# Four sublayers of attention on one core: the second layer's first values turned by DMA, some reciprocals through DRAM, x turned by TensorE

## The chip, the cores and the metric

The kernel runs on one core of a Trainium2 chip. A core has TensorE (PE, matrix products into the eight banks of PSUM), VectorE (DVE), ScalarE (ACT), GpSimd (POOL), SyncE (SP, here only a queue that issues DMAs), and sixteen DMA engines between DRAM and its memory, SBUF. The metric is the device time of one execution in microseconds, as a median of runs.

## The reference

x is 2048 tokens by 1024, in bf16. Four sublayers follow each other, A, B, A, B, and each is added to its input. The second pair uses the same weights as the first; a pair is called a layer below. Both have 32 heads of 32. A is linear attention with a learned feature map, B is softmax attention, both take a layer-normed input.

```
qkv = norm(x) @ wqkv                                # both
A:  phi(t) = [softmax(t @ w_phi), softmax(-t @ w_phi)]
    kv = phi(k)^T v ;  z = sum over tokens of phi(k)
    o  = (phi(q) kv) / (phi(q) z + 1e-6)
B:  o  = softmax(q k^T / sqrt(32)) v
x   = x + o @ wo                                    # both
```

## The kernel before

x is kept in SBUF, transposed: `xT` has the 1024 features as 8 groups of 128 partitions, and the tokens along the free dimension. Tokens are worked in 4 chunks c of 512; heads in 8 groups g of 4 heads, 128 columns. Most matmuls are made four abreast (`mm`): a 128 x 32 piece of the weights for each 32 columns of PE, four pieces beside each other, each with 512 moving columns.

Each engine's order is set when the kernel is built. Every step is an `op` of class `Sched`, with an engine, an estimated duration, the steps it depends on, its buffers and a priority; a list scheduler then runs a model of the engines and takes, for each engine, the most urgent step that is ready by its estimates. It also places all buffers in one SBUF arena and the eight PSUM banks. Where it has nothing for PE it inserts matmuls that compute nothing (`idle`, `idle_acc`), so as not to let PE stop. Tables of numbers (LATER, VQ, KP, OUT, QA, AK and others) hold the priorities. Each engine then executes its list in order, and waits at the front of it.

The stages are these. `load_x` brings x: chunk 0's features half by transposing DMAs straight into `xT`, half by plain loads that PE turns with `nc.tensor.transpose`; the other chunks come by transposing DMAs. `fold_phi` multiplies w_phi into the key weights, and later into the query weights. `layernorm` needs sums over features, that is over partitions: either 64 matmuls with a constant matrix `onesD` (every partition then holds the sums), or, for the chunks in the table FEW, 16 matmuls that leave partial sums, which two small matmuls with `selm` then add up and spread (`sums`).

Sublayer A: keys and values for each chunk give `kv` and `z`; then `a_queries`, for each chunk and half of the heads, exponentials of the two signs, their denominators and numerators, and `a_out` the out-projection. Here reciprocals occur twice: the weight between the two signs (multiplied in at line 979) and one over the denominator (line 1020). Each is one row per head, four rows in each 32 partitions, and must reach 32 partitions per head. For that the row is split in a bf16 high and low part (`split_hl`, a CAST and a SCALAR_TENSOR_TENSOR on DVE), and `spread` multiplies with `selb` or `selr`, constant matrices, into PSUM, where DVE reads it.

Sublayer B: `b_k` and `b_q` make keys and queries transposed, `b_v` makes values with tokens on the partitions (the normed x is the stationary operand, the weights move, 256 columns for the first groups of heads), and `attention` runs 32 turns, each one group of heads and one chunk of queries. Its scores go to PSUM (line 1257). A unit is one 128 keys x 512 queries tile of scores. ACT makes exponentials of three or two units at once (line 1273, 1536 or 1024 wide); for some pairs of units DVE makes them by integer and float16 arithmetic (`exp_dve`, lines 1184 to 1203). The table COUNT says how many pairs DVE takes in each of the turns. PE multiplies with the values (line 1305). The denominators go to DRAM and come back as one load that broadcasts four rows to 32 partitions each:

```
bk = dma(prio, lambda ...: nc.sync.dma_start(
    out=r_v(), in_=at_d.unsqueeze(1).to_broadcast([4, 32, C512])), [aw], [d_b], kb=600)
```

Keys of layer 1's sublayer A are made within layer 0's attention, since its turns leave the chunks of x done one after the other.

Of the kernel before, what the change touches and what calls it, by code (L numbers as in the profile page):

```python
# [23 lines left out]
DH = 32  # L24
# [45 lines left out]
class Sched:  # L70
# [99 lines left out]
    def run(self):  # L170
# [32 lines left out]
        while left:  # L203
# [108 lines left out]
SBUF_ARENA = 172 * 1024 - 256  # L312
# [3 lines left out]
LONG = {"kT", "v", "slab", "slabk", "xn", "xn1", "kvacc", "kvm", "zm", "wnat"}  # L316
MODEST = {"slabk", "xn1", "e1", "vp1", "pkf", "lnw1", "w2o"}
NUMS = 2
LATER = ((26.4, 16.7, 25.9, 7.3), (18.7, 27.9, 15.9, 13.5))
VQ = (((0, 7.1), (50.5, 3.1), (53.0, 8.9)), ((15.5, 8.4), (75.8, 14.1), (152.2, 9.9)))  # L320
FULL = 5
OUT = (35.9, 27.1)
EARLY = (2.0, 4.0)
DUE = 0.0
BOOST = 25.0
EVAC = 30.0
QA = (105.3, 4.5)
# [4 lines left out]
         "rs": 8, "pkf": 1, "cden": 2, "part": 8, "w2r": 1,  # L332
# [8 lines left out]
HOST = ((), (16,), (11, 17), (0, 11, 21), (4, 10, 17, 24))  # L341
SIDE = (2, 4)
FEW = (((0, 1, 3), (0, 1, 2)), ((0, 1, 3), (0, 1, 2)))
WHOLE = 2
WK = (0.0, 1.5)
SLABD = (1, 3)
TOK = (0.0, 0.6, 0.61, 0.62)
SLOW = 6.0
HALF = 4
KGAP = (6.2, 2.2)  # L350
LATE = 15.3
KP = (0, 39.1, 45.7, 92.0, 62.9, 125.6, 160.1, 205.2)
BO = 225
OP0 = (240.8, 265.9, 289.4)
OGAP = (2.0, 2.6, 1.9)
COUNT = ((0, 0, 1, 2, 4, 4, 4, 3, 4, 3, 3, 4, 4, 4, 4, 3, 4, 3, 3, 4, 3, 2, 1, 2, 0, 2, 4, 2, 1, 2, 3, 3),
    (2, 4, 5, 4, 4, 4, 3, 5, 4, 4, 4, 4, 4, 4, 5, 4, 3, 5, 4, 4, 4, 4, 4, 4, 4, 2, 5, 4, 3, 1, 4, 4))
PAIRS = ((), ((0, 2),), ((0, 2), (1, 2)), ((0, 1), (0, 5), (1, 3)), ((0, 1), (0, 5), (1, 1), (1, 5)),
    ((0, 1), (0, 3), (0, 6), (1, 1), (1, 5)), ((0, 1), (0, 3), (0, 6), (1, 1), (1, 3), (1, 6)))
AK = ((0, 201.9), (1, 231.9), (2, 260.5))  # L360
OUT1 = ((177.6, 3.1), (195.5, 1.0), (246.4, 1.0))


def act_us(n):
    return n / 1200 + 0.064
# [10 lines left out]
def kernel(  # L376
# [52 lines left out]
    phi_t = const.tile([P, G * P], BF16, tag="phi")  # L429
    nc.vector.memset(phi_t[:].bitcast(U32), 0)  # L430
# [45 lines left out]
    gone = []  # L476
    qd = dram_p.tile([P, 2 * G * C512], BF16, tag="qd")
# [78 lines left out]
    def load_x():  # L556
        nb, nv = sb("xnat", TB, C512)
        nat = [dma(-24.0, lambda h=h: nc.gpsimd.dma_start(
            out=nv()[:, 2 * h:2 * h + 2, :],
            in_=A_x[0, 2 * h * P:2 * h * P + 2 * P, C512:D].rearrange("(t p) f -> p t f", p=P)),  # L560
            (), [nb], q="GQ", kb=256, issue=0.75) for h in range(2)]
        for lo, hi, prio, us, kb in ((0, 1, -24.0, 1.3, 128), (1, 2, -9.0, 1.3, 400), (2, NC, -8.0, 2.0, 800)):
            last = []
            for po in range(PO if lo else PO // 2):
# [4 lines left out]
                if not lo:  # L569
                    last[-1].slack = 0.5  # L570
# [153 lines left out]
    def phi():  # L724
        return phi_t[:].rearrange("p (g n) -> p g n", g=G)
# [867 lines left out]
```

## Time and profile before

| | |
|---|---|
| median of 3 runs | 2245.05 us (2242.07 to 2246.89) |
| the profiled execution | 2247.36 us, its span 2245.1 us |
| mean granted PE clock | 0.998 |
| ACT busy | 1985.7 us, 88% of the span |
| DVE busy | 1855.9 us, 83% |
| POOL busy | 197.0 us, 9% |
| DMA | 119.67 MB, mean 53 GB/s |

In the profile PE is TensorE's matmul, PEld its weight load, which lies beside the matmuls. A row names line, engine, operation, the result and operands with their tiles, partitions x elements and type, and then, after xcount, busy us and mean ns of one; after the second bar stands the engine's idle time just before such an instruction and what ended it. SPq, ACTq and POOLq are the queues in which an engine issues DMAs. A window is a stretch of the span; its row gives its length, each engine's busy time with its count, the granted PE clock, the DMA engines' busy share and GB/s. Matmuls are pipelined: the mean duration of one is not what it adds to the time, which is read from the starts of the following rows.

### The profile page before, as it was taken

Reading aid. Unit: us, or ns where it says so; the run is one execution under the profiler, and the core shown is the slowest. Engines: PE = TensorE matmul, PEld = TensorE weight load, DVE = VectorE, ACT = ScalarE, POOL = GpSimd, SP = SyncE. Lnnn points to the kernel's source line nnn. Section 1 sums busy time; section 2 is a strip of 40 time slices with the busy share of each in tenths; the row PEclk is TensorE's granted clock in tenths of the full one; section 3 lists DMA queues with packets and bytes.
Section 4 is the critical chain, followed back from the end, with each engine's and each line's share of the span. In section 5 each row is a group of like instructions: output and inputs, shape, how many; then the busy total and the mean of one; then the engine's idle time right before and its main releaser. Section 6 shows DMA issues by size and latency. Waiting matters only on the chain.

```text
span 2245.1 us, 82636 instructions
## 1 busy us (share of the span) xinstructions
PE 2176.1 (97%) x36788; PEld 872.2 (39%) x36788; DVE 1855.9 (83%) x2761; ACT 1985.7 (88%) x1939; POOL 197.0 (9%) x299
## 2 busy tenths in 40 slices
PE   7999999999999999999999999999999999999999
PEld 4554454444333333333333444433333333333333
DVE  7986873698899889677887788799999999988968
ACT  4436669999999999999998555999999999999998
POOL 1110000000001010121124200000000000100000
PEclk9999999999999999999999999999999999999999
DMA  9220101111122221222235100111111100211111
GB/s 207 49 81 3 33 24 42 41 34 34 51 57 88 74 73 54 64 96 73 78 110 152 59 5 10 36 37 38 36 29 29 35 24 19 73 31 35 47 36 38
DMA packets 121789, 119.67 MB, mean 53 GB/s; under 512 B 57752, under 2 KB 99800, under 8 KB 121432
## 3 DMA queue, kind: packets, MB, share of 16 engines
q1 hardware_dynamic: 102392, 56.64, 10.0%
q0 software_dynamic: 17424, 56.18, 8.7%
q8 instruction: 287, 4.70, 0.9%
q10 hardware_dynamic: 1616, 1.57, 0.2%
q14 instruction: 70, 0.57, 0.1%
HBM read 79.23 MB, written 14.14 MB: 42 GB/s over the span
## 4 chain that ended last, share of the span: by engine, by line
PE 28%; ACT 23%; DVE 9%; issue 5%; DMA 1%; SPq 0%; ACTq 0%; DVEq 0%
ACT arena L1273 22%; PE psum L530 14%; PE psum L1305 6%; PE psum L1257 6%; DVE arena L1203 2%; DVE arena L1184 1%; DVE arena L1196 1%; DVE arena L1201 1%; DVE arena L1193 1%; ACT arena L823 1%; DMA arena<-arena 1%; DVE arena L1370 1%; DVE arena L1198 1%; DVE arena L1057 1%; PE psum L994 0%
## 5 line engine op out<-in xcount | busy, mean ns | idle before, releaser
L1273 ACT ACTIVATE arena<-psum 128x1536 bf16<-128x1536 f32 (+1 forms) x1366 | 1668.5, 1446 | 12.0 <-PE psum L1257 7.1
L530 PE MATMUL psum<-arena 128*32 128x512 bf16 (+1 forms) x18432 | 1058.3, 358 | 12.5 <-DVE arena L836 2.7
L530 PEld LDWEIGHTS <-arena 128*32 128x32 bf16 x18944 | 459.8, 96 | 447.2 <-issue 175.7
L1305 PE MATMUL psum<-arena 128*32 128x512 bf16 x4096 | 628.1, 383 | 4.0 <-issue 2.0
L1305 PE MATMUL psum<-arena,ones_bf 128*32 128x512 bf16 x4096 | 628.1, 383 | 0.0
L1257 PE MATMUL psum<-arena 32*128 32x512 bf16 x4096 | 536.2, 383 | 27.2 <-ACT arena L1273 22.4
L1257 PEld LDWEIGHTS <-arena 32*128 32x128 bf16 x4096 | 158.4, 91 | 555.8 <-issue 549.0
L1184 DVE TENSOR_SCALAR arena<-psum 128x512 int32<-128x512 f32 x418 | 284.5, 686 | 101.7 <-PE psum L1257 90.3
L1203 DVE SCALAR_TENSOR_TENSOR arena<-arena 128x1024 int16<-128x1024 int32 x209 | 254.7, 1218 | 5.7 <-DVE arena L1201 0.4
L1305 PEld LDWEIGHTS <-arena 128*32 128x32 bf16 x4096 | 163.2, 95 | 227.8 <-issue 177.0
L1305 PEld LDWEIGHTS <-ones_bf 128*32 128x32 bf16 x4096 | 161.3, 95 | 22.3 <-issue 7.9
L705 POOL DMA_DIRECT2D arena<-in_B_wqkv_dram x46 | 42.2, 919 | 1248.6 <-PE psum L530 302.5
L1193 DVE TENSOR_SCALAR arena<-arena 128x1024 f16<-128x1024 int16 x209 | 143.8, 690 | 4.4 <-DMA arena<-arena 0.3
L1196 DVE TENSOR_TENSOR arena<-arena 128x1024 f16<-128x1024 f16 x209 | 142.6, 684 | 4.6
L1201 DVE TENSOR_TENSOR arena<-arena 128x1024 f16<-128x1024 f16 x209 | 142.6, 684 | 3.1
L1057 DVE CAST arena<-psum 128x512 bf16<-128x512 f32 x128 | 87.7, 685 | 57.6 <-PE psum L530 57.3
L823 ACT ACTIVATE arena<-psum 128x512 bf16<-128x512 f32 x80 | 43.0, 596 | 82.6 <-PE psum L530 66.7
L827 DVE TENSOR_REDUCE arena<-arena 128x32 f32<-128x1024 bf16 x64 | 77.0, 1214 | 33.3 <-ACT arena L823 33.2
L530 PE MATMUL psum<-xT,onesD 128*32 128x512 bf16 x1144 | 103.1, 381 | 1.3 <-DVE arena L836 0.7
L1321 DVE COPY arena<-psum 128x512 f32<-128x512 f32 x126 | 86.3, 685 | 15.4 <-PE psum L1305 15.0
L1198 DVE TENSOR_SCALAR arena<-arena 128x1024 f16<-128x1024 f16 x209 | 87.9, 422 | 1.7
L836 DVE TENSOR_TENSOR arena<-psum,arena 128x1024 bf16<-128x1024 f32 x64 | 77.4, 1219 | 13.3 <-PE psum L530 9.7
(124 smaller groups left out, 1383.6 us busy)
## 6 DMA issues: line engine op xcount, KB each, us to landing
arena<-rd SPq DMA_DIRECT2D x62, 256.0 KB
arena<-in_B_wqkv_dram POOLq DMA_DIRECT2D x58, 256.0 KB, 4.1
arena<-in_B_wo_dram POOLq DMA_DIRECT2D x40, 256.0 KB, 4.4
arena<-arena SPq DMA_DIRECT2D x256, 32.0 KB
arena<-wd_k POOLq DMA_DIRECT2D x32, 256.0 KB, 5.0
arena<-in_A_wqkv_dram POOLq DMA_DIRECT2D x32, 256.0 KB, 4.6
arena<-arena SPq DMA_DIRECT2D x96, 64.0 KB
arena<-arena SPq DMA_DIRECT2D x248, 2.0 KB
```

The source lines that it names most:

```text
L530: nc.tensor.matmul(out_[ks, :], lhsT=lhsT[:, ks], rhs=rhs, start=start, stop=stop, tile_position=(0, 32 * k), skip_group_check=True)
L1057: return op("DVE", dve_us(512), lambda: nc.vector.tensor_copy(out=dst(), in_=src()), [dep], bufs, prio)
L1184: o = op("DVE", dve_us(512), lambda: nc.vector.tensor_scalar(out=x_v()[:, k, :].bitcast(I32), in0=s_v()[:, x * C512:(x + 1) * C512], scala ...
L1193: last = op("DVE", 1024 / 1920 + 0.15, lambda: nc.vector.tensor_scalar(out=z(), in0=x_v().bitcast(I16).rearrange("p a (n two) -> p a n two ...
L1196: last = op("DVE", 1024 / 1920 + 0.15, lambda: nc.vector.tensor_tensor(out=u(), in0=z(), in1=z(), op=ALU.mult), [last], [z_b, u_b], prio + ...
L1198: last = op("DVE", 1024 / 3840 + 0.15, lambda: nc.vector.tensor_scalar(out=u(), in0=u(), scalar1=POW2_C[0], scalar2=POW2_C[1], op0=ALU.mul ...
L1201: last = op("DVE", 1024 / 1920 + 0.15, lambda: nc.vector.tensor_tensor(out=u(), in0=z(), in1=u(), op=ALU.mult), [last], [z_b, u_b], prio + ...
L1203: return op("DVE", dve_us(1024), lambda: nc.vector.scalar_tensor_tensor(out=y_v().bitcast(I16), in0=x_v().bitcast(I32), scalar=128.0 / BIT ...
L1257: nc.tensor.matmul(out=s_v()[:, x * C512:(x + 1) * C512], lhsT=kT[g][1]()[r, pp, d * P:(d + 1) * P], rhs=q_of[(qc, g)][1]()[r, (pp + j // ...
L1273: ex = op("ACT", act_us(w * C512), lambda s_v=s_v, e_v=e_v, w=w: nc.scalar.activation(out=e_v(), in_=s_v()[:, 0:w * C512], func=ACT.Exp, s ...
L1305: nc.tensor.matmul(out=a_v()[col:col + 32, :], lhsT=v_v()[:, kc % 4, o:o + DH] if what == 0 else ones_bf[:], rhs=ev()[:, x * C512:(x + 1) ...
L1321: cp = op("DVE", dve_us(512), lambda t_v=t_v, a_v=a_v: nc.vector.tensor_copy(out=t_v(), in_=a_v()), [last], [a_b, t_b], prio - 4)
```

## The change

1. **x turned by TensorE.** Chunk 0 comes by four plain loads on SP (two before on POOL's queue, for half the features), and 32 transposes on PE turn it, before 16 and four transposing DMAs; DVE and ACT move the result to `xT`. The first half of the key weights comes as four loads on SP, before as one on ACT's queue. The tile for w_phi now lies in the arena, and its loads wait for its memset there.
2. **Two head groups' V transposed.** In layer 1 (TURN) the values of groups 0 and 1 are made by the new `b_vt`: weights stationary, x moving, 512 columns, as keys are. The result goes to DRAM and back by a transposing DMA, so that tokens come on the partitions. `b_v` keeps the other groups. Group 0's is evacuated by ACT, group 1's by DVE.
3. **Reciprocals of two chunks through DRAM.** For chunks 1 and 2 of both layers (WIRE) the reciprocal of the denominator goes through the new `carry` in place of `split_hl` and `spread`: four stores of four rows, then seven loads which broadcast rows to 32 partitions (a load of four rows, and 3 + 1, 2 + 2, 1 + 3, since each quarter needs the heads in a rotated order). DVE's multiply reads them from SBUF. (Set in the table's first places, the weight between the signs could go that way too; those places are empty.)
4. **`exp_dve`** uses one buffer in place of two.
5. **Norms.** FEW changes: chunk 3 of layer 0's first norm and chunk 1 of layer 1's second norm are made with the 64 matmuls.
6. **Tables.** The priorities are other numbers; COUNT sums to 88 pairs in layer 0 (before 86) and 126 in layer 1 (before 123). In layer 1 seven turns have five pairs (before five) and one has six. The arena is 1 KB larger.

```diff
-LATER = ((26.4, 16.7, 25.9, 7.3), (18.7, 27.9, 15.9, 13.5))
+LATER = ((19.6, 38.4, 22.2, 22.6), (36.6, 33.2, 21.4, 16.4))
...
-FEW = (((0, 1, 3), (0, 1, 2)), ((0, 1, 3), (0, 1, 2)))
+FEW = (((0, 1), (0, 1, 2)), ((0, 1, 2, 3), (0, 2)))
+TURN = (1,)
+WIRE = (((), (1, 2)), ((), (1, 2)))
...
-COUNT = (...
-    (2, 4, 5, 4, 4, 4, 3, 5, 4, 4, 4, 4, 4, 4, 5, 4, 3, 5, 4, 4, 4, 4, 4, 4, 4, 2, 5, 4, 3, 1, 4, 4))
+COUNT = (...
+    (2, 4, 4, 4, 5, 4, 4, 4, 4, 4, 3, 4, 3, 5, 4, 4, 5, 4, 3, 5, 4, 4, 6, 4, 4, 3, 5, 4, 5, 2, 5, 1))
...
-    phi_t = const.tile([P, G * P], BF16, tag="phi")
-    nc.vector.memset(phi_t[:].bitcast(U32), 0)
...
     def load_x():
-        nb, nv = sb("xnat", TB, C512)
-        nat = [dma(-24.0, lambda h=h: nc.gpsimd.dma_start(
-            out=nv()[:, 2 * h:2 * h + 2, :],
-            in_=A_x[0, 2 * h * P:2 * h * P + 2 * P, C512:D].rearrange("(t p) f -> p t f", p=P)),
-            (), [nb], q="GQ", kb=256, issue=0.75) for h in range(2)]
+        nb, nv = sb("xnat", TB, D)
+        nat = [dma(-24.0, lambda t=t: nc.sync.dma_start(out=nv()[:, t, :], in_=A_x[0, t * P:t * P + P, :]),
+                   (), [nb], kb=256) for t in range(TB)]
...
-            ld.append([dma(-24.0, lambda: nc.scalar.dma_start(out=nv()[:, :, 0:C512], in_=A_w[:, :, col:col + C512]),
-                           (), [nb], q="AQ", kb=1024, issue=0.7)])
...
+    def carry(r_b, r_v, dep, prio, turn):
+        at_d = wd_v[len(sent)]
+        sent.append(prio)
+        st = [dma(prio, lambda a=a: nc.sync.dma_start(out=at_d[a], in_=r_v()[32 * a:32 * a + 4, :]),
+                  [dep], [r_b], kb=8) for a in range(4)]
+        got = []
+        for a in range(4):
+            b, v = sb("wb", C512, dt=F32)
+            got.append((b, v, [st[a], b, v]))
+        r = []
+        for a, (b, v, _) in enumerate(got):
+            n = turn * a % 4
+            for lo, hi, to in ((0, 4 - n, n), (4 - n, 4, 0)):
+                if hi > lo:
+                    o = dma(prio, lambda a=a, v=v, lo=lo, hi=hi, to=to: nc.sync.dma_start(
+                        out=v()[32 * to:32 * (to + hi - lo), :],
+                        in_=at_d[a, lo:hi].unsqueeze(1).to_broadcast([hi - lo, 32, C512])), [st[a]], [b], kb=260 * (hi - lo))
...
-        k_b, k_v, k = split_hl(r_b, r_v, l4, prio)
-        for a, (b_, v_, bm) in enumerate(spread(k_b, k_v, k, prio, selr)):
+        if c in WIRE[layer][1]:
+            wide_ = carry(r_b, r_v, l4, prio, 1)
+        else:
+            k_b, k_v, k = split_hl(r_b, r_v, l4, prio)
+            wide_ = spread(k_b, k_v, k, prio, selr)
+        for a, (b_, v_, bm) in enumerate(wide_):
             o_done[4 * hf + a] = op("DVE", ...
-                out=o_v()[:, 4 * hf + a, :], in0=nums[a][1](), in1=v_(), op=ALU.mult),
-                [bm, nums[a][2]], [b_, nums[a][0], o_b], prio)
...
+    def b_vt(g, c, prio, w, vT, banks, eng):
...
+        m = mmg2(pb, pv, lambda po: ww()[:, po, h * P:h * P + P], lambda po: xv()[:, po, :], fin, wd, [xb, wb], prio)
+        a_b, a_v = sb("kt", C512)
+        cp = evac(eng, a_v, pv, m, [pb, a_b], prio)
...
+        st = dma(prio, lambda: nc.sync.dma_start(
+            out=at_v.rearrange("(t p) n -> p t n", p=P), in_=a_v().rearrange("p (t n) -> p t n", t=TB)), [cp], [a_b], kb=256)
+        ld = dma(prio, lambda: nc.sync.dma_start_transpose(out=v_v(), in_=at_v), [st], [v_b],
+                 kb=256, issue=1.3)
...
+    phi_b, phi = sb("phi", G, P)
+    phi_0 = op("DVE", 0.5, lambda: nc.vector.memset(arena[:, phi_b.at // 2:phi_b.at // 2 + G * P].bitcast(U32), 0),
+               (), [phi_b], -30.0)
```

169 lines of the change are left out of this document (106 added, 63 removed), and 1 row of the table QUOTA.

## The prediction

> **What bounds the kernel now.** I read the page's busy line first, then a table of windows cut at the stages, then the groups by shape.
>
> The busy line gives each engine's busy time, its share of the span and its instructions:
>
> ```profile
> PE 2176.1 (97%) x36788; PEld 872.2 (39%) x36788; DVE 1855.9 (83%) x2761; ACT 1985.7 (88%) x1939; POOL 197.0 (9%) x299
> ```
>
> PE at 97% looks like the bound, but PE also runs matmuls that compute nothing, where the planner had no others. The windows decide it by stage: loading and first fold; layer 0's linear attention; its softmax attention; out-projection, norm and layer 1's linear attention (here the transition); layer 1's softmax attention.
>
> ```profile
> core 0: us, PE busy (x) PEld busy (x) DVE busy (x) ACT busy (x) POOL busy (x), PEclk, DMA share, GB/s
> 0.00:31.00 31.00, 16.29 (x370) 11.23 (x374) 21.21 (x49) 14.44 (x22) 4.57 (x12) 1.00 0.92 218
> 31.00:327.00 296.00, 290.26 (x6477) 152.22 (x6469) 242.06 (x319) 157.56 (x270) 26.78 (x54) 1.00 0.23 51
> 327.00:1213.00 886.00, 863.71 (x13701) 317.68 (x13694) 695.02 (x1025) 877.28 (x746) 123.08 (x172) 1.00 0.24 68
> 1213.00:1412.00 199.00, 196.38 (x3888) 95.80 (x3880) 155.92 (x220) 116.37 (x205) 18.87 (x35) 0.99 0.12 36
> 1412.00:2235.00 823.00, 803.40 (x12249) 292.19 (x12241) 737.28 (x1142) 817.69 (x692) 23.71 (x28) 1.00 0.13 35
> ```
>
> In the two linear stages PE is busy 98 to 99% and ACT under 60%: PE's sum of matmuls is the time. In the two softmax stages ACT is busy 99% (877 of 886, 818 of 823 us) and PE 98%, part of it filler. The loading stage is neither: PE 16 of 31 us, DMA share 0.92.
>
> ```profile
> L1273 ACT ACTIVATE arena<-psum 128x1536 bf16<-128x1536 f32 x946 | 1317.1, 1573 | 9.5 <-PE psum L1257 6.4 <-PE psum L1305 1.6 <-DVE arena L1203 0.5
> L1273 ACT ACTIVATE arena<-psum 128x1024 bf16<-128x1024 f32 x420 | 433.2, 1158 | 2.6 <-PE psum L1305 0.8 <-PE psum L1257 0.7 <-issue 0.5
> L1557 PE MATMUL psum<-xT,zero 128*32 128x512 bf16 x504 | 46.5, 379 | 0.0
> ```
>
> The exponentials take 1750 us of ACT and wait 12 us in all. The zero matmuls (x504) are one of the two kinds of filler. So the prices are ACT time in softmax stages, PE time in linear ones.
>
> **The change part by part.** The sum is made against the profiled execution's 2247.4 us (span 2245.1), which is 2.3 above the median of the runs, 2245.05.
>
> *Loading.* Before, chunk 0 of x came half by four transposing DMAs and half by plain loads turned on PE; now all of it comes plain. SP's first rows, before:
>
> ```order
> L566 DMA_TRANSPOSE xT<-in_A_x_dram 128x512 x4
> L735 DMA arena<-in_A_wqkv_dram 128x2x512 x4
> L566 DMA_TRANSPOSE xT<-in_A_x_dram 128x512 x7
> L709 DMA arena<-in_A_wqkv_dram 128x2x512 x8
> L788 DMA wd_k<-arena 128x8x512
> ```
>
> and after:
>
> ```order
> L567 DMA arena<-in_A_x_dram 128x1024 x4
> L740 DMA arena<-in_A_wqkv_dram 128x2x512 x8
> L594 DMA_TRANSPOSE xT<-in_A_x_dram 128x512 x6
> L719 DMA arena<-in_A_wqkv_dram 128x2x512 x8
> L594 DMA_TRANSPOSE xT<-in_A_x_dram 128x512
> ```
>
> Four transposes left the head of the queue, and the k weights' first half, which ACT's queue carried, joined SP behind x. The timeline and the DMA list (KB each, us from issue to landing):
>
> ```profile
> 0.75 5.34 SPq L566 DMA_TRANSPOSE xT<-in_A_x_dram  x4
> 3.03 2.33 POOL L1380 DMA_DIRECT2D phi_t<-in_A_w_phi_dram  x4
> 5.45 0.15 DVE L463 TENSOR_SCALAR hl<-hl 128x1 f32<-128x1 f32 x1
> 12.04 0.69 DVE L635 TENSOR_TENSOR arena<-xT 128x1024 bf16<-128x1024 bf16 x1 [6.44 <-DMA xT<-in_A_x_dram]
> 13.67 1.03 PE L748 MATMUL psum<-ident,arena 128*128 128x128 bf16 x8
> 15.00 1.28 DVE L635 TENSOR_TENSOR arena<-xT 128x1024 bf16<-128x1024 bf16 x2
> 18.99 0.74 PE L530 MATMUL psum<-phi_t,arena 128*32 128x128 bf16 x32
> 20.98 4.58 SPq L709 DMA_DIRECT2D arena<-in_A_wqkv_dram  x8
> ```
>
> ```profile
> arena<-in_A_x_dram POOLq DMA_DIRECT2D x2, 256.0 KB, 8.1
> phi_t<-in_A_w_phi_dram POOLq DMA_DIRECT2D x4, 16.0 KB, 8.8
> ```
>
> Four issues at 0.57 us (4.58 / 8) end at 3.0, and with 8.1 us to landing x is in at 11.1 at the latest, against a last square of x that starts at 15.0. Behind it, x and the first k half are 2 MB: 9.6 us at 218 GB/s, 11.6 us with 2 us of start, against 13.67 for the first turn of k. So the front could move by 2.1 to 3.9 us. What may hold it is phi: its loads now wait for a memset that stands behind DVE's constants (5.45). With 2.33 us of issues they are out by about 8.2, and 8.8 us later, at 17.0, they are there: before the fold at 18.99, 2 us of slack. I take **−2.5**, between −4.8 (the 8.1 us were two loads among many, the wait alone was 6.44) and +1 (phi late by the gain and more).
>
> *First linear stage.* One norm is made with the full sums (64 matmuls more, 16 sum matmuls and 2 spreads fewer), and 16 spreads of reciprocals go. Rows of the timeline for the prices:
>
> ```profile
> 1274.35 4.07 PE L530 MATMUL psum<-arena 128*32 128x512 bf16 x72
> 1278.35 0.40 PE L931 MATMUL psum<-arena,selb 32*128 32x512 bf16 x4
> 1412.47 1.93 PE L530 MATMUL psum<-arena 128*32 128x256 bf16 x64
> ```
>
> 72 matmuls of 512 columns in 4.00 us are 0.0556 each, a spread is 0.10, and 64 of 256 columns in 1.87 us (to the next row's 1414.34) are 0.029 each. Norm: 64 x 0.0556 − 16 x 0.0556 − 2 x 0.2 = +2.3; spreads 16 x 0.10 = −1.6. Together **+0.7**.
>
> *Layer 0's softmax stage.* By the order ACT has four fewer 1536-wide exponentials and four more 1024-wide ones (DVE takes 88 pairs, before 86): 4 x (1.573 − 1.158) = **−1.7**.
>
> *Transition.* 288 V matmuls of 256 columns go, 96 of 512 come: −8.4 + 5.3. Its own full norm +2.3 and 16 spreads −1.6. Sum **−2.4**. The 288 moved partly into the next stage, where 512-wide matmuls rise by 160 and 256-wide ones fall by 224: +8.9 − 6.5 on PE, which the fillers cover (264 zero and 748 norm-like matmuls in that stage are 56 us).
>
> *Layer 1's softmax stage.* Six exponentials narrow (123 to 126 pairs): 6 x 0.415 = −2.5. ACT's V casts:
>
> ```profile
> L1056 ACT CAST arena<-psum 128x256 bf16<-128x256 f32 x32 | 11.9, 384 | 7.9 <-PE psum L530 7.8
> L1056 ACT CAST arena<-psum 128x512 bf16<-128x512 f32 x10 | 5.9, 598 | 17.7 <-PE psum L530 17.6
> ```
>
> Seven casts of 0.37 fewer in this stage, one of 0.60 more: −2.0, of which I count half, since they stand where ACT still waits for PE. Sum **−3.5**.
>
> *V through DRAM.* SP's row in layer 1, before:
>
> ```order
> L1070 DMA arena<-arena 64x512
> L1071 DMA arena<-arena 64x512
> L1049 DMA arena<-arena 64x256 x16
> L1070 DMA arena<-arena 64x512
> L1071 DMA arena<-arena 64x512
> ```
>
> and after, from the fourth chunk's keys on:
>
> ```order
> L1083 DMA arena<-arena 64x256 x4
> L1165 DMA vd<-arena 128x4x128 x2
> L1167 DMA_TRANSPOSE arena<-vd 128x512
> L1165 DMA vd<-arena 128x4x128
> L1167 DMA_TRANSPOSE arena<-vd 128x512
> L1104 DMA arena<-arena 64x512
> L1105 DMA arena<-arena 64x512
> L1167 DMA_TRANSPOSE arena<-vd 128x512
> ```
>
> A store and a transposing load of V (L1165, L1167) now stand between the moves of keys (L1083) and of queries (L1104, L1105), so these wait in line behind V.
>
> ```profile
> 1495.38 2.42 SPq L1049 DMA_DIRECT2D arena<-arena  x4
> 1497.21 3.08 DMA arena<-arena
> ```
>
> The trip of V is a cast 0.6, the four key moves ahead 2.4, a store's issue 0.33 and landing 3.1, a transpose's issue 1.34 (5.34 / 4) and landing 3.1: 10.9 us. Between V's evacuation and its first use the order leaves PE work of 9.5 us (chunk 2) and 11.0 us (chunk 3). I count 0, at most +5: it happens at the ramp alone.
>
> *Reciprocals through DRAM.* In chunks 1 and 2 of both layers, each half's reciprocals are stored as four rows and loaded back broadcast to 32 partitions, seven loads of 256 KB by fours, 1 MB in all. DVE's row there in layer 0, before:
>
> ```order
> L1020 TENSOR_TENSOR arena<-arena,psum 128x512 x4
> L915 CAST arena<-arena 128x512
> L1033 TENSOR_TENSOR xT<-xT,psum 128x512
> L916 SCALAR_TENSOR_TENSOR arena<-arena,hl 128x512
> L1033 TENSOR_TENSOR xT<-xT,psum 128x512 x2
> L979 TENSOR_TENSOR arena<-arena,psum 128x512 x4
> ```
>
> and after (L1054 was L1020):
>
> ```order
> L1054 TENSOR_TENSOR arena<-arena 128x512 x2
> L622 SCALAR_TENSOR_TENSOR arena<-arena,hl,psum 128x512
> L1054 TENSOR_TENSOR arena<-arena 128x512
> L679 TENSOR_TENSOR arena<-psum,arena 128x512
> L1054 TENSOR_TENSOR arena<-arena 128x512
> L701 TENSOR_TENSOR arena<-xT,arena 128x1024 x2
> ```
>
> The multiplies moved back, one by one between the next norm's steps. Each waits for a DMA, and on DVE the norm stands behind it; on PE the out-projection waits for them. The kernel has one DMA of this kind, the softmax denominators' broadcast, also four rows to 128 partitions (issues: lowest, median, highest ns). While it alone runs the windows show:
>
> ```profile
> L1364 SPq DMA_DIRECT2D arena<-rd x62: 577/582/667, 369.6 to 2223.0; - x62
> 895.47:898.21 2.74, 2.74 (x42) 0.94 (x38) 1.57 (x2) 2.74 (x4) 0.00 (x0) 1.00 0.25 96
> 507.57:510.73 3.16, 3.16 (x53) 1.19 (x56) 3.09 (x5) 3.16 (x4) 0.00 (x0) 1.00 0.23 82
> 1506.42 0.47 SPq L1362 DMA_DIRECT2D rd<-arena  x1
> 1510.38 0.59 SPq L1364 DMA_DIRECT2D arena<-rd  x1
> ```
>
> The DMA share is 0.25, four of sixteen engines, and 256 KB take 2.74 to 3.16 us. A carry's 1 MB is thus 11.0 us if the split loads keep four engines busy, and 14.0 to 16.2 if loads of three and two rows use only three and two (one engine then carries 164 packets of 2 KB where a whole load gives it 32: 5.1 x). Two carries in a row are 22 to 32 us; ahead lie 0.6 of Exp, 4.0 from the store's issue to the load's (1506.42 to 1510.38), three more stores 1.0 and a load's issue 0.6, so 28 to 38.6. The order leaves 595 matmuls of 512 columns between the first half's Exp and the first use of the last product: 33.1 us. Late per chunk −5 to +5.5, middle about +0.4, times four chunks: **+2**, bounds 0 and +22.
>
> The Trainium skill ("DMA: Bandwidth & Descriptors", section "Why a DMA increments its semaphore by 16 and not by 1") says that a hardware-queued DMA is spread over the largest number of engines up to 16 that divides the outermost sizes of both sides, the lowest-numbered ones. The share of 0.25 agrees for four rows; for three and two no run here shows it. By it the carry is the longer one, and the sum would be that of the first rival.
>
> Sum: −2.5 + 0.7 − 1.7 − 2.4 − 3.5 + 2 = −7.4, so 2240.0 in the profiled execution and **2237.5** beside the median.
>
> **The rivals.** A: *carries late* (slower). Loads of three and two rows keep few engines, both halves share the same ones, every chunk is late by 5.5 us: +22 in place of +2, so −9.4 + 22 = +12.6, 2260 profiled, **2257.5**. It loses the gain from 2.4 us a chunk on and is slower than before by over 0.2% from 3.5 us ((9.4 + 4.5) / 4). For it: DVE and PE run in order, and the last product has 2 to 6 us of matmuls ahead of its reader. Against: other matmuls (next norm, keys) can stand ahead of the waiting one, and the 33.1 us are counted without any wait in between.
>
> B: *DVE becomes the bound* (slower). One pair on DVE:
>
> ```profile
> L1184 DVE TENSOR_SCALAR arena<-psum 128x512 int32<-128x512 f32 x418 | 284.5, 686 | 101.7 <-PE psum L1257 90.3 <-ACT arena L1273 4.9 <-ACT arena L1056 2.6
> L1193 DVE TENSOR_SCALAR arena<-arena 128x1024 f16<-128x1024 int16 x209 | 143.8, 690 | 4.4 <-DMA arena<-arena 0.3
> L1196 DVE TENSOR_TENSOR arena<-arena 128x1024 f16<-128x1024 f16 x209 | 142.6, 684 | 4.6
> L1198 DVE TENSOR_SCALAR arena<-arena 128x1024 f16<-128x1024 f16 x209 | 87.9, 422 | 1.7
> L1201 DVE TENSOR_TENSOR arena<-arena 128x1024 f16<-128x1024 f16 x209 | 142.6, 684 | 3.1
> L1203 DVE SCALAR_TENSOR_TENSOR arena<-arena 128x1024 int16<-128x1024 int32 x209 | 254.7, 1218 | 5.7 <-DVE arena L1201 0.4
> 1466.00:1492.00 26.00, 25.59 (x422) 10.05 (x414) 25.86 (x42) 25.98 (x23) 0.00 (x0) 1.00 0.09 23
> ```
>
> A pair costs 2 x 0.686 + 0.690 + 0.684 + 0.422 + 0.684 + 1.218 = 5.07. Beside pairs a turn has (737.3 − 123 x 5.07) / 32 = 3.55 of DVE. A turn is 25.7 us (823 / 32), one with five pairs is 28.9 of DVE, one with six 34.0. Before, five turns had five; now seven have, and one six: 2 x 3.2 + 8.3 = 15 more that neighbours must absorb. If they can't, −7.4 + 15 = +7.6, **2252.5**. Against: in 1466 to 1492 DVE is at 25.86 of 26 and ACT still at 25.98, and L1184 idled 90 us for scores, so DVE is rather early.
>
> C: *the gains are absorbed*. If in softmax stages PE's real work is the limit and the fillers sit where nothing else fits, −1.7 and −3.5 vanish: −2.2, **2243**, no change.
>
> **How the numbers follow.** A measurement of this kernel tells 0.2%, 4.5 us, from no change. Forecast 0.62, A 0.19, B 0.06, C 0.13. Faster 0.62, same 0.13, slower 0.25. The low end takes loading at −4.8, the casts whole and no lateness: −12.7, 2232, less 2 of scatter as the runs before show: 2230. The high end is A's 2257.5.
>
> **What would show it.** In the after trace: the last square of chunk 0 before 13.5 and the first fold by 17; the transition 2 to 3 us shorter by its windows; ACT's 1536-wide exponentials at 936 without more idle time; L1054 waiting for its loads under 3 us a chunk. Idle PE over 3 us ahead of L530 in chunks 1 and 2, released by L1054, would prove A; ACT waiting for L1203 would prove B; either makes the forecast wrong, as does V's transpose (L1167) showing up as releaser of the values' matmuls beyond the first turns.

## The result and the profile after

The changed kernel takes 2277.35 us (2275.86 to 2279.54, 4 runs) against 2245.97 us (2242.07 to 2250.86) in the same session: a ratio of 1.0136, 95% interval [1.0121, 1.0150]. It is slower by 31 us; the forecast was 2237.5, and its range ended at 2257.5. The profiled execution took 2279.54 us, its span 2277.7.

The page's busy line after, then the windows cut at the same stages (first and last exponential of the two softmax stages):

```profile
PE 2184.5 (96%) x36540; PEld 868.8 (38%) x36540; DVE 1868.1 (82%) x2782; ACT 1984.2 (87%) x1927; POOL 195.4 (9%) x297
```

```profile
31.00:340.00 309.00, 290.43 (x6383) 153.05 (x6382) 235.61 (x304) 154.95 (x264) 26.91 (x55) 0.98 0.26 61
340.00:1227.00 887.00, 862.18 (x13664) 315.70 (x13662) 699.95 (x1039) 876.71 (x747) 126.16 (x177) 1.00 0.25 70
1227.00:1442.00 215.00, 200.24 (x3732) 92.94 (x3731) 153.26 (x212) 116.36 (x199) 15.48 (x28) 0.97 0.18 49
1442.00:2267.00 825.00, 802.25 (x12160) 288.65 (x12155) 750.27 (x1166) 814.36 (x686) 23.74 (x28) 1.00 0.14 37
```

Most of the loss is in the two linear stages, where the reciprocals are: the first ends at 340.3 in place of 327.1, the transition takes 215.3 in place of 199.8. PE has about as much to do there as before, but stands idle, and its granted clock is 0.98 and 0.97. The softmax stages are longer by 1.0 and 2.3 us.

VectorE's waits in each of these two stages (us in total, times, longest):

```profile
DVE arena L1054 <- DMA arena<-wd__121: 17.2, 8, 7.6
```

```profile
DVE arena L1054 <- DMA arena<-wd__121: 16.2, 10, 7.1
```

L1054 is the multiply by the reciprocal, wd the DRAM tile of the trips. One such stop in the timeline, on VectorE, ScalarE and PE:

```profile
277.63 0.69 DVE L1054 TENSOR_TENSOR arena<-arena 128x512 bf16<-128x512 f32 x1 [7.59 <-DMA arena<-wd__121]
```

```profile
278.35 0.59 ACT L1032 COPY arena<-psum 128x512 f32<-128x512 f32 x1 [6.10 <-DVE arena L1054]
278.83 0.59 ACT L678 COPY arena<-psum 128x512 f32<-128x512 f32 x1
```

```profile
278.99 1.04 PE L539 MATMUL psum<-arena 128*32 128x512 bf16 x8 [5.09 <-ACT arena L1032]
```

This is chunk 2 of layer 0, the third multiply of its first half. VectorE waits 7.6 us for the load. ScalarE's L1032 copies a numerator of the second half out of PSUM into one of four buffers (the planner's quota for "ns" is four), and the one that it gets is what the multiply still has to read; so ScalarE waits 6.1 us, with the norm's copy (L678) behind it, and PE 5.1 us behind ScalarE. Here it is the third of the chunk's eight products that stops the row, not the last.

The longest stop of layer 1 is of another kind:

```profile
1392.88 0.69 DVE L1054 TENSOR_TENSOR arena<-arena 128x512 bf16<-128x512 f32 x1 [7.07 <-DMA arena<-wd__121]
```

```profile
1394.23 1.21 PE L1024 MATMUL psum<-arena 32*32 32x512 bf16 x16 [6.19 <-DVE arena L1009]
```

This is the seventh product of chunk 2. Behind it in VectorE's row stands L1009, the multiply by the weight between the signs, and PE's next numerators (L1024) wait 6.2 us for that. Here the order of VectorE's own row passes the wait on.

The chain of waits around the first of these stops shows what the trip is made of:

```profile
264.07 16.36 DMA wd__121<-arena
...
280.56 0.58 SPq L956
...
284.56 12.66 DMA arena<-wd__121
```

The second half's four stores, 8 KB each, need 16.4 us to land: they stand in SyncE's queue behind the first half's seven loads. Only then can the second half's loads be issued, and the last of them takes 12.7 us more.

Both stops fall on trips that did not have the DMA engines to themselves. Counted from the first packet to the last, six of the eight trips take 13 to 15 us for their loads; chunk 2's first half in layer 0 takes some 20 and its second half in layer 1 18.2. Beside these two, GpSimd's loads of sublayer B's weights moved 1.31 and 1.05 MB, beside the others 0.25 at most. No run took these loads away, so what they cost is not known.

### The profile page after: what moved, and what is told of

Its sections match the earlier page's. It is cut to its first block, busy times and chain, and to the rows that moved or that the text cites. A ratio compares the mean times of both kernels' runs of the same rounds, so it can differ in the third digit from the quotient of the medians.

```text
span 2277.7 us, 82286 instructions
## 1 busy us (share of the span) xinstructions
PE 2184.5 (96%) x36540; PEld 868.8 (38%) x36540; DVE 1868.1 (82%) x2782; ACT 1984.2 (87%) x1927; POOL 195.4 (9%) x297
## 4 chain that ended last, share of the span: by engine, by line
PE 47%; ACT 25%; DVE 13%; issue 8%; DMA 6%; SPq 1%; ACTq 0%; DVEq 0%
PE psum L539 26%; ACT arena L1335 23%; PE psum L1367 10%; PE psum L1319 9%; DMA arena<-wd__121 3%; DVE arena L1238 2%; DVE arena L1257 2%; DMA wd__121<-arena 1%; DVE arena L1247 1%; DVE arena L1250 1%; ACT arena L828 1%; DVE arena L1255 1%; DMA arena<-arena 1%; DVE arena L1432 1%; DVE arena L1252 1%
## 5 line engine op out<-in xcount | busy, mean ns | idle before, releaser
L539 PE MATMUL psum<-arena 128*32 128x512 bf16 (+2 forms) x18688 | 1071.4, 358 | 31.3 <-ACT arena L977 6.0
L1238 DVE TENSOR_SCALAR arena<-psum 128x512 int32<-128x512 f32 x428 | 291.3, 684 | 70.8 <-PE psum L1319 62.1
L1257 DVE SCALAR_TENSOR_TENSOR arena<-arena 128x1024 int16<-128x1024 int32 x214 | 259.9, 1215 | 2.1
L1250 DVE TENSOR_TENSOR arena<-arena 128x1024 f16<-128x1024 f16 x214 | 146.0, 682 | 5.5 <-ACT arena L1335 0.2
L1255 DVE TENSOR_TENSOR arena<-arena 128x1024 f16<-128x1024 f16 x214 | 145.8, 681 | 3.0
L1383 DVE COPY arena<-psum 128x512 f32<-128x512 f32 x126 | 86.0, 683 | 17.1 <-PE psum L1367 16.9
```

Source lines behind the costliest of these rows:

```text
L539: nc.tensor.matmul(out_[ks, :], lhsT=lhsT[:, ks], rhs=rhs, start=start, stop=stop, tile_position=(0, 32 * k), skip_group_check=True)
L1238: o = op("DVE", dve_us(512), lambda: nc.vector.tensor_scalar(out=x_v()[:, k, :].bitcast(I32), in0=s_v()[:, x * C512:(x + 1) * C512], scala ...
L1250: last = op("DVE", 1024 / 1920 + 0.15, lambda: nc.vector.tensor_tensor(out=u(), in0=z(), in1=z(), op=ALU.mult), [last], [z_b, u_b], prio + ...
L1255: last = op("DVE", 1024 / 1920 + 0.15, lambda: nc.vector.tensor_tensor(out=u(), in0=z(), in1=u(), op=ALU.mult), [last], [z_b, u_b], prio + ...
L1257: return op("DVE", dve_us(1024), lambda: nc.vector.scalar_tensor_tensor(out=y_v().bitcast(I16), in0=x_v().bitcast(I32), scalar=128.0 / BIT ...
L1383: cp = op("DVE", dve_us(512), lambda t_v=t_v, a_v=a_v: nc.vector.tensor_copy(out=t_v(), in_=a_v()), [last], [a_b, t_b], prio - 4)
```

## The experiments

Times are medians, with the ratio to the kernel before of the same session. In these sessions the kernel before was at 2244.95 to 2247.07. Lengths of stages are of one profiled execution each.

**Without the trips.** `WIRE = (((), ()), ((), ()))`.

> The changed kernel with all reciprocals spread by TensorE again, everything else of the change kept. Theory 1 (the trips of reciprocals through DRAM cost the whole loss, some 29 us: 11 us more in the first linear stage, 18 us in the transition): 2240 to 2250 us, no wait of VectorE's last multiply for a DMA, and PE without idle stretches over 2 us in both linear stages. Theory 2 (V through DRAM, the full norms and the new tables carry a good part, the trips only some 10 us): over 2262 us, with the idle stretches of PE still there behind ScalarE or the norm.

2257.56 us, ratio 1.0047 [1.0032, 1.0063]: between the two. The trips' idle stretches are gone (PE's waits for VectorE in the first linear stage are under 1 us each), so 20 us of the loss went with them. But 11 us are left, in two of the stages as follows:

```profile
327.00:1216.00 889.00, 860.99 (x13688) 316.88 (x13686) 699.03 (x1038) 877.96 (x746) 125.11 (x169) 1.00 0.24 67
1216.00:1420.00 204.00, 200.44 (x3804) 92.37 (x3796) 157.68 (x223) 115.50 (x200) 20.30 (x37) 0.99 0.15 43
```

The first linear stage is as long as before (327.2), the three later ones are longer (by 3.2, 4.2 and 4.6 us), although ScalarE has less to do. Taking the trips out gave the planner other durations, and it made another order: in the transition stand 48 more of the matmuls of 512 columns made four abreast than in the changed kernel. So this run does not price the trips alone, which I had taken it to do.

**The trips alone, added to the kernel before** (`carry` and its two calls).

> The kernel before with only the trips of reciprocals through DRAM added, in chunks 1 and 2 of both layers, and before's own tables. Theory 1: 2246 plus 22 to 32, so 2268 to 2278 us, with waits of the multiply for the loads of 15 us or more in each layer. Theory 2: under 2258 us. A third way (the new tables had made room for the trips, and without them the loss is larger): over 2282 us.

2283.90 us, ratio 1.0167 [1.0150, 1.0184]: +37 us, just in the range of the third way. Both linear stages show it: 12 us more in the first, 16 in the transition. The planner made a new order here too, so the 37 us, like the 20 of the run before, are not the trips' alone; that the new tables made room for the trips is not shown by it.

**Stores in another queue.** `nc.sync.dma_start(out=at_d[a], ...)` becomes `nc.gpsimd.dma_start`.

> The changed kernel with the four stores of each trip issued by GpSimd, so that they do not stand in SyncE's DMA queue behind the seven loads of the half before. Theory 1a (the second half's stores stuck for 8 to 16 us behind the first half's loads make it late): the stores land within 4 us, each second trip is 6 to 12 us shorter, 2255 to 2268 us. Theory 1b (the loads themselves, 14 to 18 us for each trip on few engines, are what is late, and second loads queue behind first loads anyway): second trips end at most 3 us earlier, 2272 to 2279 us.

2271.77 us, ratio 1.0113 [1.0095, 1.0132]: 1b, or nearly. The stores now land in time, but the loads of the second half still stand behind those of the first: in chunk 1 the last load lands at 245.2 where it landed at about 247.5. The stuck stores were a consequence more than a cause. (This run was planned anew as well, so the 6 us that it gained are not purely theirs.)

**One-row loads.** The seven loads of a trip become sixteen, of one row to 32 partitions each:

```diff
-    for lo, hi, to in ((0, 4 - n, n), (4 - n, 4, 0)):
-        if hi > lo:
-            o = dma(... out=v()[32 * to:32 * (to + hi - lo), :],
-                in_=at_d[a, lo:hi].unsqueeze(1).to_broadcast([hi - lo, 32, C512]) ..., kb=260 * (hi - lo))
+    for lo, hi, to in ((0, 4 - n, n), (4 - n, 4, 0)):
+        for j in range(lo, hi):
+            o = dma(... out=v()[32 * k:32 * k + 32, :], in_=at_d[a, j:j + 1].to_broadcast([32, C512]) ..., kb=260)
```

> The changed kernel with each trip's seven loads of one to four rows replaced by sixteen loads of one row each, so that the outermost size of both sides is 32. Theory 1b (few DMA engines carry a trip): the one-row loads run on all engines, DMA share near 1 while they run, a trip's loads last 9 to 11 us (sixteen issues of 0.6) in place of 14 to 18, stores are no longer stuck, 2250 to 2265 us. Rival (the length of the trip does not come from the number of engines but from packets of 2 KB read over and over from the same DRAM rows): the loads last 14 us or longer again, 2274 us or more.

2245.83 us, ratio 0.9995 [0.9986, 1.0004]: better than expected. The same 512 packets of 2 KB, by more than twice the DMAs, and the loss of 31 us is gone. Two windows, both while a trip's loads run; the first is of the changed kernel in chunk 1 (second half), the second of this run at the same place:

```profile
240.00:247.00 7.00, 7.00 (x133) 3.80 (x126) 5.55 (x7) 2.54 (x6) 0.00 (x0) 1.00 0.16 59
```

```profile
229.18:238.30 9.12, 9.12 (x176) 4.38 (x168) 8.49 (x9) 9.05 (x19) 0.00 (x0) 1.00 0.40 117
```

0.16 of sixteen DMA engines is 2.6 engines, at loads of three and two rows; one-row loads come to 0.40, not near 1 as expected: the issues on SyncE (8.9 us for these sixteen) set the pace. The trip's loads last 9.1 us from the first packet to the last, in the changed kernel 14.2 at this place. The rival, by which the packets themselves made the length, is out.

The packets of these two trips, the changed kernel's first, tell more:

```profile
DMA packets 560, 1.08 MB, mean 66 GB/s; under 512 B 46, under 2 KB 46, under 8 KB 558
```

```profile
DMA packets 769, 1.07 MB, mean 99 GB/s; under 512 B 256, under 2 KB 256, under 8 KB 768
```

Small packets come 46 to seven loads and 256, sixteen each, to sixteen; a load of four rows in the kernel before, at its share of 0.25, has 4. If there is one for each engine that a load uses, 46 is 4 + (3 + 16) + (2 + 2) + (16 + 3): a load of n rows is on n engines, and a load of one row on sixteen. That reading fits the shares; the trace does not name the engines.

**The same, with all orders kept.** The planner changed its order a little in that run. Here each planned load issues its rows as separate DMAs within one step; the rows of PE, VectorE, ScalarE and GpSimd are the changed kernel's, instruction by instruction, and only SyncE's differ:

```diff
-    o = dma(prio, lambda ...: nc.sync.dma_start(<n rows>), [st[a]], [b], kb=260 * (hi - lo))
+    def rows(...):
+        for j in range(lo, hi):
+            nc.sync.dma_start(out=v()[32 * k:32 * k + 32, :], in_=at_d[a, j:j + 1].to_broadcast([32, C512]))
+    o = dma(prio, rows, [st[a]], [b], kb=260 * (hi - lo))
```

> The changed kernel, in which each load of n rows is issued as n loads of one row, inside the same step of the planner: the orders of TensorE, VectorE, ScalarE and GpSimd are the changed kernel's to the last instruction, and only SyncE's row differs (sixteen issues of a trip in place of seven). If the number of DMA engines that carry a trip is the whole cause of the loss by the trips, this comes to the time of the earlier run with one-row loads, 2243 to 2249 us, with PE's idle stretches of 5 and 6 us and the half clock behind them gone. If that run owed part of its gain to an order that the planner changed, 2252 us or more.

2240.73 us, ratio 0.9975 [0.9966, 0.9985]: 2 us under the range expected. This is faster than before, by 6 us, and 36.6 us under the changed kernel with the same orders. The stages and VectorE's wait of the first linear one:

```profile
31.00:328.00 297.00, 286.72 (x6414) 154.08 (x6410) 235.70 (x306) 154.72 (x266) 26.88 (x55) 1.00 0.28 64
328.00:1208.00 880.00, 858.40 (x13649) 315.03 (x13638) 699.08 (x1039) 875.09 (x745) 126.81 (x177) 1.00 0.25 70
1208.00:1405.00 197.00, 194.11 (x3732) 89.96 (x3732) 152.23 (x212) 116.36 (x200) 15.27 (x28) 1.00 0.19 54
1405.00:2228.00 823.00, 800.96 (x12156) 288.25 (x12155) 750.32 (x1166) 813.58 (x686) 23.74 (x28) 1.00 0.14 37
```

```profile
DVE arena L1056 <- DMA arena<-wd__121: 1.4, 2, 0.8
```

L1056 is the multiply here. Its waits fell from 17.2 to 1.4 us, and the clock stays whole. This run carries the argument: the loads' shape alone makes the loss.

**One-row loads in the kernel before.**

> The kernel before with only the trips of reciprocals added, by one-row loads. If the number of DMA engines was the whole cause of the loss by the trips: within 4 us of before, 2242 to 2249 us, against 2283.9 us with the loads of up to four rows. If before's order leaves the trips too little time anyway: over 2252 us.

2258.99 us, ratio 1.0059 [1.0046, 1.0072], 25 us under the run with loads of up to four rows, but 14 over before. The first linear stage is 1.7 us shorter (325.4), as the spreads' price said; the transition is 5.3 longer and layer 0's softmax stage 6.8. In the transition some 80 more matmuls of 256 columns stand and PE idles 3.6 us more. The time is in the second range, but not for the reason given there: the loads are no longer late (VectorE waits 1.1 us for them in the first linear stage, 20.5 with loads of up to four rows). What is left is put down to the new order; no run shows it by itself. What sets the softmax stage back was not followed up.

**The planner told the truth.** Loads `kb=(1000, 1600, 2200, 2800)[a]`, the second half's stores `kb=1600`.

> The changed kernel with its seven loads as they are, but the planner told a trip's length as measured: loads 7, 10, 13 and 16 us after the stores in place of 3 to 7, stores of the second half 10 us in place of 2. If the loss is a loss of order (VectorE and PE stand in line at a multiply that the planner put too early, while other work was there): 2245 to 2262 us, with under 8 us of the multiply's waits for the loads in each layer. If there is no other work to put there, the trip is on the path in any order: 2268 us or more.

2330.50 us, ratio 1.0375 [1.0360, 1.0390]: in the range of the second expectation, but 53 us above the changed kernel, which neither foresaw.

```profile
31.00:368.00 337.00, 304.79 (x6482) 156.19 (x6482) 236.27 (x304) 156.40 (x268) 25.70 (x53) 0.94 0.24 56
```

The first linear stage is 28 us longer than even the changed kernel's and PE idles 32 us in it. VectorE still waits 16.8 and 16.9 us for the loads in the two linear stages. A likely reason is that the planner, with the numerators held in four buffers, found nothing else to put there and moved later steps behind the trip; this was not followed up. These durations alone gave no better order.

**Fillers at PE's two long idle stretches.** The changed kernel, with `mm(psum[bank 2], onesD, xT, ...)` 20 and 24 times ahead of the waiting steps.

> The changed kernel as it is, with matmuls that compute nothing (into a bank of PSUM that is free there) placed in PE's row at its two long idle stretches: 20 groups of four before the one of 5.1 us, 24 before the one of 6.2 us, 4.4 and 5.3 us of work; all orders are otherwise the same. In the changed kernel's trace the granted clock is 0.50 for some 7 and 5 us behind these two. If the idle time causes it, the half clock is gone, PE's own work behind them takes 3.6 and 2.7 us less, and the whole falls by 3 to 7 us, to 2270 to 2274. If the clock falls for another cause, or the work behind waits for the trips anyway, 2276 us or more.

2279.65 us, ratio 1.0142 [1.0127, 1.0157]: nothing gained. At the first place the edit did what it should. The changed kernel behind its idle stretch of 5.1 us, and this run at the same work:

```profile
281.00:283.00 2.00, 1.30 (x16) 0.55 (x19) 1.42 (x2) 1.95 (x4) 0.00 (x0) 0.50 0.14 51
283.00:285.00 2.00, 2.00 (x24) 0.83 (x20) 1.70 (x2) 1.77 (x5) 0.00 (x0) 0.50 0.38 124
```

```profile
283.00:285.00 2.00, 1.70 (x32) 0.93 (x35) 1.11 (x2) 2.00 (x5) 0.00 (x0) 1.00 0.18 66
285.00:287.00 2.00, 2.00 (x44) 1.10 (x37) 2.00 (x2) 2.00 (x5) 0.00 (x0) 1.00 0.35 123
```

At this place the idle time causes the half clock, and the filler avoids it. But from the step behind it to the first exponential it is 59.0 us here (283.3 to 342.3) and 58.6 in the changed kernel (281.7 to 340.3). PE gets through its work sooner and then idles 2.1 us that it did not idle before, for VectorE's L1054 and L921, and L1054 waits 3.2 us for loads there in place of 1.6: what the clock gives is waited away, for the trips in part. At the second place the edit misfired, since the filler itself had to wait:

```profile
1392.90 7.47 PE L539 MATMUL psum<-xT,onesD 128*32 128x512 bf16 x96 [7.50 <-DVE arena L1009]
```

It ran behind the wait, at the half clock, and cost what it took. What the half clock is worth in the transition is thus open.

**The softmax stage of layer 1.** With the trips out of the way that stage gains nothing (825 us where 822 were): ScalarE's work fell by 3 us and its idle time rose by 5.6. Two places, of the run with one-row loads:

```profile
1424.15 4.30 ACT L1335 ACTIVATE arena<-psum 128x1024 bf16<-128x1024 f32 x4 [3.70 <-PE psum L1319]
```

```profile
1981.05 3.71 ACT L1335 ACTIVATE arena<-psum 128x1536 bf16<-128x1536 f32 x3 [2.86 <-PE psum L1319]
```

The first is the ramp, the first turns of attention, where PE makes group 1's V between the values' matmuls. The second lies in the turn with six pairs, in which VectorE works without a pause from 1959 to 1984. So the six pairs were set to five in one run, V made by rows (`TURN = ()`) in another, both in a third:

> The changed kernel with one-row loads in the trips (as in the run with sixteen loads, 2245.8 us), and the one turn of layer 1 with six pairs on VectorE set to five. Theory (VectorE is the bound in that one turn: there it works without a pause and ScalarE idles 2.9 us for scores): the idle of 2.9 us goes, one exponential widens by 0.4 twice, 2242 to 2245 us. Rival (that idle is a matter of the row of PE, not of VectorE's load): it stays, 2246 us or more.

2244.07 us, ratio 0.9996 [0.9988, 1.0005]. The idle of 2.9 us is gone, and two of 1.1 stand elsewhere; the stage is 824.8.

> The changed kernel with one-row loads, and layer 1's V of groups 0 and 1 made by rows as before instead of transposed. Theory (V through DRAM pays in the transition, where 288 matmuls of 256 columns left, and takes back 3.7 us at the first turns of attention, where PE makes group 1's V beside the values' matmuls): transition 3 to 5 us longer, ScalarE's idle of 3.7 us at the ramp gone, 2245 to 2249 us. Rival (V through DRAM is the reason that the softmax stage gained nothing): under 2243 us.

2248.05 us, ratio 1.0009 [1.0000, 1.0018]. The transition is 199.3 (1.9 longer), the ramp's idle 1.7 in place of 3.7, the stage 824.5.

> The changed kernel with one-row loads, the six-pair turn set to five, and V by rows as before: the two places where ScalarE idled in layer 1's softmax stage (3.7 us at the ramp, 2.9 us in the six-pair turn) are both taken away. If these two were what the stage's expected gain went into, the stage is 820 to 822 us and the whole 2240 to 2244 us, faster than before. If idle time appears in other turns instead, the stage stays at 824 or more and the whole at 2245 or more.

2243.20 us, ratio 0.9980 [0.9971, 0.9989]. The stage is 820.7 as expected:

```profile
1412.00:2233.00 821.00, 801.59 (x12288) 291.44 (x12289) 743.52 (x1155) 816.07 (x692) 23.44 (x28) 1.00 0.13 35
```

Whether V through DRAM pays is not settled: without it the run with six pairs is 2.2 us slower and the run with five 0.9 faster (by the ratios 0.14% slower and 0.16% faster), and the intervals and the replanned rows (888.6 against 886.6 in layer 0's softmax stage) are of that size.

**The version that beats both.** The orders kept, one-row loads, five pairs in place of six.

> The changed kernel with each load of n rows issued as n loads of one row within the planner's step (2240.7 us), and the six-pair turn set to five. The idle of 2.9 us of that turn goes against two exponentials wider by 0.4: 2237 to 2241 us, if the first softmax stage keeps its 880 us. If taking a pair away moves the order elsewhere for the worse (as it seemed to between 2245.8 and 2244.1, where the turn gained 2.9 and the stage nothing): 2241 to 2245 us.

2238.25 us, ratio 0.9963 [0.9951, 0.9975], the stage at 821. It is faster than the kernel before and than the changed one; its interval overlaps that of the run with six pairs.

```profile
1404.00:2225.00 821.00, 799.71 (x12138) 287.62 (x12138) 746.49 (x1159) 814.52 (x686) 24.00 (x28) 1.00 0.14 37
```

## Why the prediction was wrong

**The step that failed** is the term for the reciprocals through DRAM, +2 of 0 to +22. With the orders kept, the loads' shape costs 36.6 us (2277.35 against 2240.73). Five things in that step were off.

- *The deadline.* I counted 595 matmuls, 33.1 us, from the first half's Exp to the first use of the chunk's last product. In chunk 2 of layer 0 the first reader that matters is nearer. The numerators' four buffers must be free for the second half, so the first half's third product is due early: in the run with all orders kept it starts 13.3 us behind Exp, nearly without a wait (1 us at most for each product). In the changed kernel it came after 20.1 us. My own bounds gave a single trip at least 8.2 us for three of its four quarters and 6.2 ahead of them, 14.4: held against 13.3, they would have told "late" even with four busy engines. In chunk 2 of layer 1 the stop is at the seventh product, which came 34.8 us behind Exp and, with the orders kept, after 26.1. The chunks' last products came after 34.6, 39.8, 36.0 and 37.6 us, within the 28 to 38.6 of the prediction but for one, and waited under 1 us each: the products ahead of them had been held up already.
- *The middle.* It was taken over −5 to +5.5 us a chunk, as if a trip that comes early gave time back. With early trips counted as nothing, the same range gives some 1.4 us a chunk, near +6 in all (an estimate from those bounds alone): still far too little.
- *The engines.* I took the middle between four busy engines and fewer. The window above has 2.6 engines at loads of three and two rows, and a trip that ran by itself took 14.2 us for its loads (233.3 to 247.5), the low end of "14.0 to 16.2". The rule quoted from the Trainium skill ("DMA: Bandwidth & Descriptors", section "Why a DMA increments its semaphore by 16 and not by 1") held: this case's share agrees with it, and one-row loads, whose outermost sizes are 32 on both sides, are spread more widely, as it says (share 0.40, sixteen small packets each).
- *The queue.* That the second half's small stores land only behind the first half's loads (16.4 us) was not thought of; by the run with the stores elsewhere it is worth about 6 us (2271.8 against 2277.4), in another order.
- *Other loads.* That GpSimd's weight loads share the engines with a trip was not thought of either. The two trips beside them took some 20 and 18.2 us and made the two longest stops; with the orders kept and one-row loads the first of these two is again the longest trip, some 14 us where the others take 8 to 10.

**Rival A** was right in its mechanism, its place and its sign, and idle stretches of PE over 3 us were the sign that I had named, though the one of 5.1 us stands behind ScalarE's L1032 and the one of 6.2 us, ahead of L1024, behind L1009, not behind L1054 itself. Its price, four times 5.5, was too low, since it put the lateness at the end of the chunk only, when it strikes at several products on the way, and the half clock behind long idle stretches was not in it. The first linear stage lost 13.2 against before and the transition 15.5; with 0.6 and −2.8 in the run with the orders kept, the trips made 12.6 and 18.3 of that. Layer 0's softmax stage is another 6 us longer than in that run (886.6 against 880.4), with the same rows and 5 us more idle time on ScalarE. The two executions stay within 1 us of each other up to 981; then the changed kernel falls back 2.7 us at its first stretch of half clock there and 3.0 at the second:

```profile
986.18:989.46 3.28, 3.28 (x25) 0.70 (x24) 0.25 (x1) 2.57 (x2) 1.30 (x3) 0.50 0.95 326
1112.34:1115.76 3.42, 3.42 (x30) 0.88 (x31) 2.57 (x3) 1.94 (x2) 0.56 (x1) 0.50 0.23 81
```

The execution with the orders kept has none. The run with fillers, with the same rows but for those, has one, at another place (1192.4), and 882.9 us. So these 6 us go with the clock of that one execution; why it fell there, and whether the loads' shape had a part in it, was not found.

**The other terms**, read from the two runs with one-row loads (orders kept; replanned), with the tail of about +0.7 left aside. They are of single executions: in layer 0's softmax stage that of the kernel before also has two such stretches of 3.4 us at half clock (from 925.3 and 1150.5), the one with the orders kept none and the replanned one a single one, so a few us between the two columns are not the change's.

| term | predicted | measured |
|---|---|---|
| loading and first linear stage | −2.5 + 0.7 | +0.6; −1.6 |
| layer 0's softmax stage | −1.7 | −5.2; +0.9 |
| transition | −2.4 | −2.8; −2.4 |
| layer 1's softmax stage | −3.5 | +0.6; +2.7 |

The transition's sum was right to half a us, in part by luck: V's share of it was −3.1, and taking V through DRAM away gave back only 1.9 and 1.1. Loading moved further than predicted at the front and gave it back: x is squared by 10.6 where the last square ended at 16.3, the first fold starts at 14.40, not 18.99, and waits for w_phi as foreseen (w_phi came by 14.4, not 17.0; my 2 us of slack were counted against the old time of a fold that my own sum moves forward); the first exponential of keys comes 7.3 us earlier, and by 150 us only 1.6 are left.

```profile
8.14 2.49 DVE L645 TENSOR_TENSOR arena<-xT 128x1024 bf16<-128x1024 bf16 x4
14.40 0.94 PE L539 MATMUL psum<-arena 128*32 128x128 bf16 x32 [0.30 <-DMA arena<-in_A_w_phi_dram]
```

Layer 1's softmax stage went the way of rival B and of the bound on V, in small: ScalarE's work did fall by 3 us, and the ramp (3.4 to 3.7 us, of which 1.7 stand without V's trip too; within the +5 that I allowed and did not count) and the six-pair turn (2.9) took it back. VectorE is the bound in one turn, not in the stage: setting six to five there gave 1.9 us of the stage, 823.0 to 821.1. The sum without the trips, −9.4, measures −6.2 with the orders kept.

## What to carry to other kernels

A transfer moved off an engine is only free up to its nearest reader, and that reader can be a buffer: look for who must reuse what the waiting instruction reads, not only for who uses its result. A broadcast load whose outermost size is 2, 3 or 4 occupies few DMA engines and stops whatever stands behind it in the queue; split by rows, with 32 outermost, the same bytes came in 8 to 10 us (one trip in some 14) in place of 13 to 20, and the change that had lost 1.4% won 0.25%. In a kernel whose order a planner sets, price an edit with all orders kept, as here by issuing within one step; runs that replanned moved other stages by up to 7 us. Before a stage's difference of some 3 us is explained, look for a stretch of half clock in one of the two executions.

## What the runs showed of the hardware

PE's granted clock halves at an idle stretch of 5.1 us (0.50 from 279 to past 285) and at one of 6.2 us (0.50 from 1394 to 1398):

```profile
1332.00:1336.20 4.20, 0.61 (x16) 0.21 (x12) 1.07 (x2) 1.70 (x4) 0.00 (x0) 1.00 0.08 28
1336.20:1339.00 2.80, 2.80 (x55) 1.68 (x58) 2.80 (x4) 2.80 (x7) 0.00 (x0) 1.00 0.30 110
...
1394.20:1396.00 1.80, 1.77 (x24) 0.61 (x27) 1.53 (x3) 0.66 (x3) 0.00 (x0) 0.50 0.05 18
1396.00:1398.00 2.00, 2.00 (x24) 0.72 (x20) 2.00 (x5) 1.00 (x3) 0.00 (x0) 0.50 0.00 0
```

A stretch of 3.6 us (from 1332.5) left it whole. In the same execution one of 1.75 us did not, behind matmuls of 33 columns; nor did one of 2.1 us up to 986.2, whose row stands above (0.50, 986.18 to 989.46):

```profile
62.23:63.98 1.75, 0.00 (x1) 0.00 (x1) 0.76 (x2) 0.00 (x0) 0.00 (x0) 1.00 0.00 0
63.98:64.45 0.47, 0.47 (x22) 0.29 (x21) 0.07 (x1) 0.00 (x0) 0.00 (x0) 1.00 0.00 0
64.45:67.86 3.41, 3.41 (x94) 2.60 (x96) 2.92 (x5) 2.83 (x6) 0.00 (x0) 0.50 0.29 98
```

So the length of a stretch does not settle it in these traces. The stretches at half clock last 3.4, 6.8 or 10.2 us in all of them, but for those that the end of an execution cuts off. The Trainium skill ("TensorE: Matmul & The Clock Gate", section "Part 1: The HAM clock gate (the "warmup" mystery)") gives about 3.4 us as the window of idle time after which the clock halves. The 5.1 and 6.2 agree with that, and the 3.6 shows that just over one window does not always do it; the 1.75 is shorter than the window and halved the clock all the same, and here the measurement decides.
